# Eight zero products instead of ten at the start, and the half tile ahead of the single tile

## The chip, the cores and the metric

The kernel runs on one core of a Trainium2 chip. The metric is the device time of one execution in microseconds, the median over several executions. The engines are TensorE (PE; its weight loads are shown as PEld), VectorE (DVE), ScalarE (ACT), GpSimd (POOL) and SyncE (SP). SP and POOL issue most DMAs. The engines run their own instruction streams and wait for each other through semaphores.

## The reference

Two blocks follow each other. The first is sparse attention over 8 sequences of 576 tokens and 8 heads of 64; half of the heads look at the last 32 positions, the other half at positions of the same class modulo 32. The second is a layer of 8 experts with one expert for each token. A token takes the expert of its own largest logit, or that of the token before it where a local gate says so:

```python
for s in range(S):
    fresh_e = int(np.argmax(logits[b, s]))
    e = fresh_e if s == 0 or local_gate[b, s] < 0.5 else prev_e
    prev_e = e
    h = np.maximum(x[b, s] @ w1[e], 0.0)      # 512 -> 1024
    out[b, s] = p[e] * (h @ w2[e])            # 1024 -> 512, p = softmax of the logits
```

So the number of tokens of each of the eight experts depends on the data; there are 4608 in all. Everything is float32.

## The kernel before, in words

**Attention.** `attention` (line 148) walks over 8 sequences and 4 pairs of heads. In each step it loads q and k of a pair (SP's queue, line 169), multiplies scores on PE (`scores`, L264), takes the exponential on ACT (L268), masks on DVE (L275), multiplies by the values on PE (L288) and divides on DVE (L301, L302). The results are stored to a table of rows in HBM. Ahead of the first scores, `busy(WARM)` (line 186) issues products of a tile of zeros with itself, 128 x 512 in bf16 (L184); they use nothing but the zeroed tile, and nothing uses their results. `WARM` is 10 (line 59).

**Routing.** A `Router` turns the logits into lists of rows: for each expert the numbers of its tokens in tiles of 128. All experts have at least four such tiles in the code path ("two pairs"); what an expert has beyond these 512 rows is counted in halves of 64 rows, and this count, from 0 to 6, is read into registers as the number of an arm.

**Experts.** `Experts.run` (line 797) goes over the experts in order. Two tiles are done together as a pair, in a scheme with seven products in place of eight (`pair_hidden`, L835, and `pair_output`, L871). `rest` (line 999) does the second pair of an expert, and in the middle of it switches to the arm. The arm builds a list `more` of what is still to do: pairs, a single tile of 128 rows (`single`, L926 for the first layer, L937 for the second), a half tile of 64 rows (`half`, L947 for the first layer, L957 to transpose its result, L967 for the second layer). An arm with number 3 has a single and a half tile.

The order of work in an arm is written out by hand. It gathers the rows of the first entry (`gather`, L765, an indirect DMA issued by POOL, from the table in HBM into one tile in SBUF), ends the pair (`part2`), which issues two scatters of results on POOL (L791), and then, for each entry, issues the gather of the entry after it into the same SBUF tile, and does the entry:

```python
for i, r in enumerate(more):
    then = more[i + 1] if i + 1 < len(more) else nxt
    if i + 1 < len(more):
        self.gather(then)
```

Each of `part2`, `single` and `half` also prepares the entry that follows it, its `nxt`: ACT multiplies the gathered rows by their gate (`scale`, L771), PE transposes them (`turn`, L778), ACT copies the result from PSUM (L779), and for a pair DVE makes four differences (`row_sums`, L787). In `single` the scale stands ahead of the first layer, and the turn between the two layers. In `half` the scale stands ahead of the first layer as well; the turn is made in two calls, one for each tile of a pair that follows, the first after the first layer and the second after the transposes L957. ACT does the relu of a first layer (L822), and for the half tile DVE does the other half of it (L953); ACT copies the second layer's result (L938 for the single tile, L973 for the half tile), and a scatter on POOL writes it. SP loads the weights of the expert after the next one (L724, L727) when the last use of a weight tile is over. `steps` are lists of sums of weights on DVE (L732) that are worked off between the parts.

## Time and profile before

| what | value |
|---|---|
| median of 3 runs | 678.8 us (678.07 to 679.64) |
| profiled execution | 679.77 us, its span 678.0 us |
| PE busy | 661.1 us, 97% of the span |
| PE weight loads | 569.3 us |
| DVE, ACT, POOL busy | 353.8, 195.4, 118.4 us |
| single tile's layers L926 and L937 | 29.2 and 28.4 us in all, four tiles |
| half tile's layers L947 and L967 | 14.6 and 14.7 us in all, four half tiles |
| products of zeros, L184 | 5.9 us, 15 of them in the trace, ten of which stand at the start |

The span runs from the first to the last instruction of one profiled execution; the execution's own time has some 1.8 us around it. A row of the timeline gives start, busy time, engine, line, operation, the tiles written and read and the number of instructions merged; in brackets stands how long the engine was idle before it, and who ended that.

### The profile page before, as it was taken

The page shows a single profiled execution, that of the slowest core. Times are in us where ns is not written, and L with a number is a line of the kernel's source. Part 1 is how long each engine was busy: PE and PEld are TensorE (multiplying, and loading weights), DVE is VectorE, ACT ScalarE, POOL GpSimd, SP SyncE. Part 2 cuts the span into 40 slices and gives each one's busy share as a digit, 9 for nine tenths or more (in the row PEclk, how much of TensorE's full clock was granted, in tenths as well). Part 3 has the DMA queues.
Part 4 walks back from the last instruction along what each step waited for, and adds up shares of the span by engine and source line. Part 5 has one row for each costly group of instructions (what it writes and reads, how often), then busy time and mean ns, then how long its engine had stood idle before and what let it go on. Part 6 is the DMA issues. An engine that isn't in the chain of part 4 may idle for free.

```text
span 678.0 us, 14758 instructions
## 1 busy us (share of the span) xinstructions
PE 661.1 (97%) x6019; PEld 569.3 (84%) x6020; DVE 353.8 (52%) x783; ACT 195.4 (29%) x364; POOL 118.4 (17%) x144
## 2 busy tenths in 40 slices
PE   9999999999999999999999999999999999999994
PEld 6887888878999999499979989996799899699493
DVE  6558876856884447126523664560256456422131
ACT  3545445353311221321222222222222222221220
POOL 3431010112022023012011201301011112121001
PEclk9999999999999999999999999999999999999998
DMA  9999877755321082171045226201711712021001
GB/s 323 408 380 325 278 251 254 274 168 196 122 64 54 17 300 66 39 270 57 27 156 170 65 75 241 67 18 40 268 45 54 256 55 74 34 56 42 18 9 37
DMA packets 35800, 95.83 MB, mean 141 GB/s; under 512 B 4790, under 2 KB 11702, under 8 KB 35628
## 3 DMA queue, kind: packets, MB, share of 16 engines
q1 hardware_dynamic: 27164, 71.41, 30.0%
q0 software_dynamic: 7936, 22.38, 10.3%
q8 instruction: 66, 1.08, 0.7%
q14 instruction: 106, 0.87, 0.4%
q10 hardware_dynamic: 528, 0.10, 0.1%
HBM read 74.69 MB, written 19.69 MB: 139 GB/s over the span
## 4 chain that ended last, share of the span: by engine, by line
PE 57%; DMA 1%; issue 1%; DVE 1%; ACT 0%; POOL 0%; POOLq 0%; ACTq 0%
PE lps L835 22%; PE mps L871 21%; PE mps L937 4%; PE mps L967 2%; PE lps L947 2%; PE lps L926 2%; PE xps L778 2%; DMA x<-xd,gi 1%; PE lps L957 0%; POOL out_dram L791 0%; DVE h L958 0%; ACT y L973 0%; ACT x L771 0%; DVE y L823 0%; DVE wt L732 0%
## 5 line engine op out<-in xcount | busy, mean ns | idle before, releaser
L791 POOL DMA_INDIRECT out_dram<-y,tab x40 | 46.2, 1154 | 350.0 <-DVE y L823 245.4
L835 PE MATMUL lps<-tt,ws 128*128 128x128 f32 x768 | 91.5, 275 | 0.0
L835 PEld LDWEIGHTS lps<-tt,ws 128*128 128x128 f32 x768 | 88.5, 192 | 0.2
L871 PE MATMUL mps<-wt,k 128*128 128x256 f32 x384 | 85.7, 380 | 0.0
L871 PEld LDWEIGHTS mps<-wt,k 128*128 128x128 f32 x384 | 72.8, 190 | 9.9
L835 PE MATMUL lps<-xt,w1t 128*128 128x128 f32 x512 | 63.0, 276 | 3.0 <-ACT y L973 1.9
L835 PEld LDWEIGHTS lps<-xt,w1t 128*128 128x128 f32 x512 | 60.4, 192 | 6.5 <-ACT y L973 3.7
L823 DVE TENSOR_TENSOR h<-lps,u 128x512 f32<-128x512 f32 x48 | 33.1, 691 | 57.6 <-PE lps L835 57.4
L871 PE MATMUL mps<-w2t,h 128*128 128x256 f32 x256 | 60.5, 379 | 0.0
L268 ACT ACTIVATE e<-sps 128x576 f32<-128x576 f32 (+1 forms) x64 | 41.6, 651 | 54.8 <-PE sps L264 53.9
L765 POOL DMA_INDIRECT x<-xd,gi x40 | 42.0, 1050 | 81.4 <-PE lps L835 39.0
L871 PEld LDWEIGHTS mps<-w2t,h 128*128 128x128 f32 x256 | 47.4, 190 | 5.8
L264 PE MATMUL sps<-qk 64*128 64x96 f32 (+2 forms) x704 | 50.4, 280 | 0.9 <-issue 0.8
L822 ACT ACTIVATE h<-h 128x512 f32<-128x512 f32 x48 | 30.2, 630 | 70.1 <-DVE h L823 65.2
L264 PEld LDWEIGHTS sps<-qk 64*128 64x128 f32 (+2 forms) x704 | 42.2, 183 | 8.2 <-issue 6.9
L822 ACT ACTIVATE h<-lps 128x512 f32<-128x512 f32 (+1 forms) x28 | 15.6, 562 | 82.2 <-PE lps L835 66.1
L823 DVE TENSOR_TENSOR u<-lps,p 128x512 f32<-128x512 f32 x16 | 11.1, 692 | 53.4 <-PE lps L835 32.9
L771 ACT ACTIVATE x<-x 128x512 f32<-128x512 f32 (+1 forms) x40 | 27.1, 717 | 33.6 <-DMA x<-xd,gi 21.9
L779 ACT COPY xt<-xps 128x512 f32<-128x512 f32 (+1 forms) x38 | 20.3, 565 | 51.1 <-PE xps L778 51.1
L835 PE MATMUL lps<-tt,w1t 128*128 128x128 f32 x256 | 31.3, 275 | 0.0
L835 PE MATMUL lps<-xt,ws 128*128 128x128 f32 x256 | 31.3, 275 | 0.0
L871 PE MATMUL mps<-w2t,k 128*128 128x256 f32 x128 | 30.4, 380 | 0.0
(238 smaller groups left out, 959.3 us busy)
## 6 DMA issues: line engine op xcount, KB each, us to landing
w1t<-in_w_dram SPq DMA_DIRECT2D x7, 2048.0 KB
w2t<-in_w_dram SPq DMA_DIRECT2D x7, 2048.0 KB
qk<-in_qkl_dram SPq DMA_DIRECT2D x16, 592.0 KB
qk<-in_qks_dram SPq DMA_DIRECT2D x16, 576.0 KB
vl<-in_vf_dram SPq DMA_DIRECT2D x8, 780.0 KB
vs<-in_vg_dram SPq DMA_DIRECT2D x8, 639.8 KB
xd<-xl SPq DMA_DIRECT2D x12, 288.0 KB
xd<-xs SPq DMA_DIRECT2D x48, 63.0 KB
```

Of the source, the lines that this page charges most:

```text
L264: nc.tensor.matmul(ps[0:m, h, c:c + w], lhsT=t[r, S + j * width:S + j * width + m], rhs=t[r, j * width:j * width + w], start=(u.local and ...
L268: nc.scalar.activation(e[0:kb, :, 0:n], ps[0:kb, :, 0:n], Act.Exp, bias=0.0, scale=1.0 / DH ** 0.5)
L765: self.nc.gpsimd.indirect_dma_start(out=r.x[0:r.m, i], out_offset=None, in_=self.xd[0:r.rows], in_offset=bass.IndirectOffsetOnAxis(ap=r.gi ...
L771: self.nc.scalar.activation(r.x[0:r.m, i, 0:D], r.x[0:r.m, i, 0:D], Act.Copy, scale=r.gate[i][0:r.m])
L778: self.nc.tensor.transpose(ps[:, kk, 0:r.m], r.x[0:r.m, i, kk * P:(kk + 1) * P], self.ident[0:r.m, 0:r.m])
L779: self.nc.scalar.copy(out=r.xt[:, i, :, 0:r.m], in_=ps[:, :, 0:r.m])
L791: s = self.nc.gpsimd.indirect_dma_start(out=self.out, out_offset=bass.IndirectOffsetOnAxis(ap=r.si[i][0:r.m], axis=0), in_=y[0:r.m, i], in ...
L822: relu = lambda o, i: nc.scalar.activation(o, i, Act.Relu)
L823: add = lambda o, i, p: nc.vector.tensor_tensor(o, p, i, op=Alu.add)
L835: nc.tensor.matmul(ps[:, f], lhsT=m[:, kk, f * P:(f + 1) * P], rhs=v[:, kk], start=(start and f == 0 and kk == 0), stop=(kk == 1), skip_gr ...
L871: nc.tensor.matmul(ps[:, 0:256], lhsT=m[:, f], rhs=v[:, f], start=(start and f == 0), stop=(f == 3), skip_group_check=True)
L937: nc.tensor.matmul(ps, lhsT=h[f // 4][:, f % 4], rhs=w.w2[:, f], start=(f == 0), stop=(f == FK - 1))
```

## The change

The number of products of zeros ahead of the first scores goes from 10 to 8. In an arm with both, the list `more` holds the half tile ahead of the single tile. Since a half tile can now be followed by an entry of one tile, `turn` with `only=1` does nothing where the entry has no second tile.

```diff
-WARM = 10
+WARM = 8
...
     def turn(self, r, bank, only=None):
         if r is not None:
-            for i in range(r.n) if only is None else [only]:
+            for i in range(r.n) if only is None else range(only, min(only + 1, r.n)):
...
                 if arm > 3:
                     more.append(rows(spot, e, (4, 5)))
+                if arm % 2:
+                    more.append(rows(spot, e, (4 + arm // 2,), HALF))
                 if arm % 4 > 1:
                     more.append(rows(spot, e, (4 + arm // 4 * 2,)))
-                if arm % 2:
-                    more.append(rows(spot, e, (4 + arm // 2,), HALF))
```

## The prediction

> **What bounds the kernel now.** I read the page first, then the timeline of TensorE (PE) over the expert part, then the timelines of POOL and ACT at the same places, because the page's averages hide which wait ends last where the change works.

> ```profile
> span 678.0 us, 14758 instructions
> ...
> PE 661.1 (97%) x6019; PEld 569.3 (84%) x6020; DVE 353.8 (52%) x783; ACT 195.4 (29%) x364; POOL 118.4 (17%) x144
> ```

> PE works 97% of the span, so what lengthens PE's own sequence, or puts a hole in it, lengthens the kernel; work on other engines counts only where PE waits for it. The change touches two places. The first is the start (PE, PEld and ACT rows of the timeline; columns are start, busy us, engine, line, operation):

> ```profile
> 1.37 4.45 PE L184 MATMUL vps<-warm 128*128 128x512 bf16 x10 [1.37 <-DVE warm L179]
> 5.75 3.43 PE L264 MATMUL sps<-qk 64*128 64x96 f32 x48
> ...
> 6.89 1.32 ACT L268 ACTIVATE e<-sps 128x576 f32<-128x576 f32 x2 [4.23 <-PE sps L264]
> ```

> Ten products of zeros start 0.427 us apart; the first scores follow without a hole. The trace's semaphore events have the first qk load complete at 4.62 us, so the scores wait for the zeros, not for their data.

> The second place is an arm with a single tile and a half tile. PE's timeline shows L926/L937 (single) followed by L947/L957/L967 (half) three times, at 262.7, 455.1 and 617.4 us: experts 0, 4 and 7. Expert 4 in full, PE rows first, then POOL and ACT:

> ```profile
> 455.11 0.60 PE L778 MATMUL xps<-ident,x 128*128 128x128 f32 x4
> 455.55 1.89 PE L871 MATMUL mps<-w2t,k 128*128 128x256 f32 x8
> 457.27 7.31 PE L926 MATMUL lps<-xt,w1t 128*128 128x128 f32 x64
> 464.84 0.46 PE L778 MATMUL xps<-ident,x 64*128 64x64 f32 x4 [0.25 <-ACT x L771]
> 465.32 7.13 PE L937 MATMUL mps<-w2t,h 128*128 128x512 f32 x16
> 472.38 3.65 PE L947 MATMUL lps<-w1t,xt 128*64 128x512 f32 x16
> 475.97 0.66 PE L778 MATMUL xps<-ident,x 128*128 128x128 f32 x4
> ...
> 477.93 3.67 PE L967 MATMUL mps<-w2t,h 128*64 128x256 f32 x32
> 482.07 2.05 PE L835 MATMUL lps<-xt,w1t 128*128 128x128 f32 x16 [0.46 <-ACT y L973]
> ```
> ```profile
> 458.71 1.27 POOL L791 DMA_INDIRECT out_dram<-y,tab  x1 [1.15 <-DVE wt L732]
> 460.28 0.94 POOL L765 DMA_INDIRECT x<-xd,gi  x1 [0.30 <-issue]
> ...
> 464.06 0.72 ACT L771 ACTIVATE x<-x 64x512 f32<-64x512 f32 x1 [7.67 <-DMA x<-xd,gi]
> ```

> The second tile of the arm is gathered behind the pair's last scatter, at 460.28; ACT can scale its rows only at 464.06, 3.78 us later, and ends at 464.78. PE turns them at 464.84. That chain starts when the pair's last product ends and is done 7.5 us after it, and the single tile's first layer (L926, 7.15 us from start to the next operation when nothing stops it, at 340.14) covers all but 0.25 us. **The cover is the length of the first tile's first layer.**

> Two more stretches give me durations: a half tile alone after a pair (expert 6) and a single tile alone (expert 2).

> ```profile
> 582.34 0.46 PE L778 MATMUL xps<-ident,x 64*128 64x64 f32 x4
> ...
> 584.66 3.65 PE L947 MATMUL lps<-w1t,xt 128*64 128x512 f32 x16
> 588.24 0.66 PE L778 MATMUL xps<-ident,x 128*128 128x128 f32 x4
> ```
> ```profile
> 347.29 1.04 PE L778 MATMUL xps<-ident,x 128*128 128x128 f32 x8
> 348.16 7.03 PE L937 MATMUL mps<-w2t,h 128*128 128x512 f32 x16
> 355.03 1.17 PE L835 MATMUL lps<-xt,w1t 128*128 128x128 f32 x9
> ```

> [...] 427 ns per product of zeros, and at the end the granted clock falls to 0.50 at 671.7 us, 3 us after PE's last product. [...]

> **The change, part by part.**

> *Two products of zeros fewer.* 2 x 0.427 = 0.85 us less ahead of the scores, so they start at about 4.9, after the load (4.62). But [...] the pairs of score products come 0.11 us apart only from 6.2 us on, twice that before. The first unit is six pairs; with one 0.32 us start and the rest at 0.22 it ends near 6.4 instead of 6.84, and its exp starts 0.45 us earlier. The chain behind it (exp, mask, values) moves with it: the loads used at 7.59, 9.11 and 11.0 complete at 6.47, 8.36 and 9.95, at least 0.75 us early. I take **-0.45**, between 0 (a load late next) and -0.85 (clock already up).

> *Half before single (three arms).* Only the order changes: each instruction and transfer keeps its size. The turn's new bound lets the half tile's two calls serve a next of one tile: the first turns it, the second issues nothing. Other arms keep their order. From the turn of the first tile in the pair (call it A: 262.69, 455.11, 617.37):
> - L947 starts at A+2.32 (expert 6: 582.34 to 584.66) and the next turn is wanted 3.58 later (584.66 to 588.24): A+5.90.
> - The single tile's gather stands at the same place on POOL: after both scatters. The scatters wait for the same DVE additions, so it is issued at about A+5.2 for experts 0 and 4 (5.17 before), and A+4.96 for expert 7, whose scatter takes 1.0 instead of 1.27 us. The gather has 128 rows instead of 64: gathers of 128 rows complete 3.0 to 3.8 us after issue in the trace, those of 64 rows 2.9 to 3.7, so I add nothing. Issue to scale was 3.67, 3.78 and 2.98 us, the scale 0.72, the turn 0.05 later: A+9.67, A+9.78, A+8.71.
> - PE stands for **3.77, 3.88 and 2.81 us**. Queued behind the turn are L957, L967 and the whole single tile; on ACT the half tile's relu (L822) stands behind the scale, so it isn't early either, and DVE's half of the relu follows ACT's.
> - From the turn: 1.8 to L967 (1.96 before; DVE's relu is up to 0.2 earlier relative to it), 3.6 for L967, 7.15 for L926, 0.87 and 6.87 for turn and L937 (expert 2's rows): 20.3. The next pair then starts at A+29.95, 30.06 and 28.99; it was 26.85, 26.96 and 26.54. Per expert **+3.1, +3.1 and +2.45**.
> - In that sum are the gains: the 0.46 us wait for ACT's y copy at the end of a half tile goes in all three (a single tile's end shows none at 355.03), the 0.25 and 0.14 us waits of the old second turn go, and the half tile's turn in the pair is 0.05 us shorter.
> - SP's weight loads follow the last use of the weights: w1 is free 1.6 us earlier before the next pair, w2 0.5 us later; neither was waited for by PE in these stretches: nothing. Expert 0's remaining weight sums on DVE now run beside L967 and L926: nothing.

> Sum: 3.1 + 3.1 + 2.45 - 0.45 = **+8.2 us**. The profiled execution took 679.77 (span 678.0, 1.77 around it), 0.97 over the median of 678.8; I put the sum on the median: **687.0**, and about 686.2 for a span.

> **Rivals.**
> 1. *The clock falls in the hole (28%).* A stand of 3.8 us is longer than the 3.0 us of idleness after which the clock fell at the end[...]. For: the clock's record at 671.7; against: no hole of this length lies inside the span. One time 688.7, two 690.4.
> 2. *A faster transfer (14%).* If the gather takes expert 7's 2.98 us everywhere and POOL its shorter scatter, the holes shrink by about 1 us each in experts 0 and 4, or somewhat more if the single's rows come sooner: 683 to 685.
> 3. *The hole is covered after all, faster (4%).* Place: the turn at A+5.90. If the scaled rows are there by then, only gains remain: 26.18 against 26.85, 26.96 and 26.54, so -1.8, and -0.45 at the start: 676.5. It decides at 0.7 us from gather issue to scaled rows, where 3.7 to 4.5 were seen; or if the gather went ahead of the scatters, which its order in the queue excludes.
> 4. *The new order isn't executed (2%).* Then only the start counts: 678.35. Three stretches in the timeline speak against it.

> **How the numbers follow.** The main case has 52%, own range 685.2 to 688.2 (holes 0.5 us either way, start 0 to -0.85). About 0.2%, 1.4 us, is what a measurement can tell from no change. Slower by more: main, 1 and 2, 94%; within: 2%; faster: 4%. Range 683.5 to 690.0: it leaves out rival 3, two clock falls, and the lower part of rival 2.

> **What would show it.** PE rows in expert 4: L778 (64 rows), L871, L947, then L778 with a wait of 3 to 4 us put down to ACT x L771 or the DMA behind it; L967, L926, L937, and L835 with no wait for ACT y. PE's busy time is hardly changed, its share falls by a point. First scores near 4.9, first exp near 6.45. Wrong if the wait is under 2 us, if the gather is issued before the scatters, or if L947 outlasts the scale.

## The result and the profile after

The changed kernel takes 693.4 us, median of 6 runs (692.45 to 694.4), against 678.8 us for 6 runs of the kernel before (677.38 to 679.64): a ratio of 1.0223, 95% interval 1.0212 to 1.0234. It is 14.6 us slower. The forecast was slower, by 8.2 us, 687.0 in all, and its range ended at 690.0: the sign was right, the size was not. The profiled execution took 694.4 us, its span 692.7.

The page after, first lines and the slice line of the granted clock (one digit for each fortieth of the span, in tenths):

```profile
span 692.7 us, 14737 instructions
...
PE 667.3 (96%) x6017; PEld 573.9 (83%) x6018; DVE 353.9 (51%) x783; ACT 195.8 (28%) x364; POOL 116.5 (17%) x144
...
PEclk9999999999999998999999999998999999998998
```

The span is 14.7 us longer, but PE's busy time also grew, by 6.2 us (661.1 before), though PE has no more work than before (two products of zeros fewer). Three slices ahead of the last one show an 8. Work that takes longer at a lower clock is a second loss beside the waiting.

The waits of PE after (engine, line, releaser: us in all, times, longest) show the first loss:

```profile
PE xps L778 <- ACT x L771: 10.1, 3, 3.4
PE mps L967 <- DVE h L958: 1.6, 3, 0.5
```

Three times PE stands for 3.4 us ahead of a turn, as the main case said; the wait of 0.5 us ahead of L967 was not foreseen. Here is one whole arm (expert 0), on PE's timeline, then POOL's and ACT's row of the second tile's rows:

```profile
261.85 0.46 PE L778 MATMUL xps<-ident,x 64*128 64x64 f32 x4
262.24 1.99 PE L871 MATMUL mps<-w2t,k 128*128 128x256 f32 x8
264.16 3.65 PE L947 MATMUL lps<-w1t,xt 128*64 128x512 f32 x16
271.24 1.12 PE L778 MATMUL xps<-ident,x 128*128 128x128 f32 x4 [3.43 <-ACT x L771]
272.15 1.06 PE L957 MATMUL lps<-ident,h 128*128 128x128 f32 x4
273.73 5.11 PE L967 MATMUL mps<-w2t,h 128*64 128x256 f32 x32 [0.52 <-DVE h L958]
278.76 7.41 PE L926 MATMUL lps<-xt,w1t 128*128 128x128 f32 x64
...
293.75 1.95 PE L835 MATMUL lps<-xt,w1t 128*128 128x128 f32 x16
```
```profile
267.08 0.99 POOL L765 DMA_INDIRECT x<-xd,gi  x1 [0.30 <-issue]
```
```profile
270.46 0.72 ACT L771 ACTIVATE x<-x 128x512 f32<-128x512 f32 x1 [7.75 <-DMA x<-xd,gi]
```

The order is the predicted one: the gather of the single tile is issued 5.23 us after the arm's first turn, ACT scales 3.38 us later, and L947 had ended at 267.8. But L967 takes 5.11 us, where it took 3.67 before, and the second turn and the transposes L957 are slower too (1.12 and 1.06 us, where they took 0.66 and 0.90). The same stretch cut at the changes of the clock (columns: stretch, length, busy time and instructions of PE, PEld, DVE, ACT and POOL, then the granted clock, DMA share and GB/s):

```profile
262.50:266.43 3.93, 3.93 (x20) 2.02 (x21) 3.30 (x7) 0.21 (x1) 2.14 (x2) 1.00 0.18 67
266.43:269.84 3.41, 1.38 (x8) 0.21 (x4) 0.00 (x0) 0.00 (x0) 1.33 (x2) 1.00 0.48 151
269.84:271.24 1.40, 0.00 (x1) 0.00 (x1) 0.00 (x0) 0.78 (x2) 0.00 (x0) 0.50 0.03 12
271.24:276.67 5.43, 4.91 (x22) 3.29 (x24) 3.25 (x6) 1.18 (x3) 0.00 (x0) 0.50 0.00 0
276.67:280.00 3.33, 3.33 (x31) 2.36 (x28) 0.00 (x0) 1.09 (x3) 0.08 (x1) 1.00 0.00 0
```

At 269.84, while PE stands, the granted clock falls to 0.50; it comes back at 276.67, 6.83 us later. The other two arms do the same: down at 467.82 and 635.07, up 6.83 us later each time. The mean granted clock of the six executions is 0.981 to 0.986, against 0.994 to 0.997 in all twenty of the kernel with fewer zeros alone (below), so the clock fell in the others too.

From the arm's first turn to the next pair's first product:

| arm of expert | before | after | added |
|---|---|---|---|
| 0 | 26.85 | 31.90 | 5.05 |
| 4 | 26.96 | 32.11 | 5.15 |
| 7 | 26.54 | 32.25 | 5.71 |

Together 15.9 us. Outside the arms the profile after gets some 1.5 us back: it reaches the first arm 0.84 us earlier (261.85 against 262.69; only 0.04 of this comes from the start, most of the rest from shorter waits between 60 and 145 us), two waits of 0.56 us elsewhere are gone, and one of 0.47 is new. That leaves 14.4 of the span's 14.7; the last 0.3 was not followed.

At the start, PE's and ACT's rows after:

```profile
1.36 3.59 PE L184 MATMUL vps<-warm 128*128 128x512 bf16 x8 [1.36 <-DVE warm L179]
4.89 4.25 PE L264 MATMUL sps<-qk 64*128 64x96 f32 x48
```
```profile
6.53 0.65 ACT L268 ACTIVATE e<-sps 128x576 f32<-128x576 f32 x1 [3.87 <-PE sps L264]
```

The scores start at 4.89, the first exponential at 6.53 (4.9 and 6.45 were forecast). The values of the first unit are done at 10.62, though, against 10.66 before: in this execution the clock rose at 7.02 instead of 6.16, which takes the lead back.

### The profile page after: what moved, and what is told of

Read it like the earlier page. It is cut to its first block, busy times and chain, and to the rows that moved or that the text cites. A ratio compares the mean times of both kernels' runs of the same rounds, so it can differ in the third digit from the quotient of the medians.

```text
span 692.7 us, 14737 instructions
## 1 busy us (share of the span) xinstructions
PE 667.3 (96%) x6017; PEld 573.9 (83%) x6018; DVE 353.9 (51%) x783; ACT 195.8 (28%) x364; POOL 116.5 (17%) x144
## 3 DMA queue, kind: packets, MB, share of 16 engines
q8 instruction: 66, 1.08, 0.7%
## 4 chain that ended last, share of the span: by engine, by line
PE 92%; DVE 2%; DMA 2%; issue 1%; ACT 1%; POOL 0%; POOLq 0%; SPq 0%; DVEq 0%; ACTq 0%
PE lps L835 29%; PE mps L871 28%; PE sps L264 6%; PE vps L288 6%; PE lps L926 4%; PE mps L937 4%; PE tps L330 3%; PE mps L967 3%; PE xps L778 3%; PE sps L258 2%; DMA x<-xd,gi 1%; PE tps L354 1%; PE vps L184 1%; DMA xd<-xl 1%; PE tps L382 1%
## 5 line engine op out<-in xcount | busy, mean ns | idle before, releaser
L791 POOL DMA_INDIRECT out_dram<-y,tab x40 | 46.1, 1152 | 368.7 <-DVE y L823 247.4
L835 PE MATMUL lps<-tt,ws 128*128 128x128 f32 x768 | 91.7, 275 | 0.5 <-issue 0.5
L835 PEld LDWEIGHTS lps<-tt,ws 128*128 128x128 f32 x768 | 88.6, 192 | 0.7 <-issue 0.5
L871 PE MATMUL mps<-wt,k 128*128 128x256 f32 x384 | 85.7, 380 | 0.0
L871 PEld LDWEIGHTS mps<-wt,k 128*128 128x128 f32 x384 | 72.8, 190 | 9.9
L835 PEld LDWEIGHTS lps<-xt,w1t 128*128 128x128 f32 x512 | 60.6, 192 | 4.0 <-issue 2.7
L835 PE MATMUL lps<-xt,w1t 128*128 128x128 f32 x512 | 62.7, 276 | 0.5 <-ACT y L973 0.5
L871 PE MATMUL mps<-w2t,h 128*128 128x256 f32 x256 | 60.5, 379 | 0.0
L268 ACT ACTIVATE e<-sps 128x576 f32<-128x576 f32 (+1 forms) x64 | 41.7, 651 | 53.2 <-PE sps L264 52.2
L765 POOL DMA_INDIRECT x<-xd,gi x40 | 40.2, 1005 | 79.9 <-PE lps L835 44.0
L871 PEld LDWEIGHTS mps<-w2t,h 128*128 128x128 f32 x256 | 47.4, 190 | 5.8
L264 PE MATMUL sps<-qk 64*128 64x96 f32 (+2 forms) x704 | 51.0, 283 | 0.1
L822 ACT ACTIVATE h<-h 128x512 f32<-128x512 f32 x48 | 30.2, 630 | 70.1 <-DVE h L823 67.1
L264 PEld LDWEIGHTS sps<-qk 64*128 64x128 f32 (+2 forms) x704 | 43.1, 186 | 8.2 <-issue 6.0
L822 ACT ACTIVATE h<-lps 128x512 f32<-128x512 f32 (+1 forms) x28 | 15.8, 565 | 92.9 <-PE lps L835 68.3
L787 DVE TENSOR_TENSOR tt<-xt 128x256 f32<-128x256 f32 x32 | 13.5, 421 | 52.2 <-ACT xt L779 52.2
L771 ACT ACTIVATE x<-x 128x512 f32<-128x512 f32 (+1 forms) x40 | 27.1, 717 | 35.4 <-DMA x<-xd,gi 23.0
L835 PE MATMUL lps<-tt,w1t 128*128 128x128 f32 x256 | 31.3, 275 | 0.0
L835 PE MATMUL lps<-xt,ws 128*128 128x128 f32 x256 | 31.3, 275 | 0.0
```

What stands on the lines that cost most here:

```text
L264: nc.tensor.matmul(ps[0:m, h, c:c + w], lhsT=t[r, S + j * width:S + j * width + m], rhs=t[r, j * width:j * width + w], start=(u.local and ...
L268: nc.scalar.activation(e[0:kb, :, 0:n], ps[0:kb, :, 0:n], Act.Exp, bias=0.0, scale=1.0 / DH ** 0.5)
L765: self.nc.gpsimd.indirect_dma_start(out=r.x[0:r.m, i], out_offset=None, in_=self.xd[0:r.rows], in_offset=bass.IndirectOffsetOnAxis(ap=r.gi ...
L771: self.nc.scalar.activation(r.x[0:r.m, i, 0:D], r.x[0:r.m, i, 0:D], Act.Copy, scale=r.gate[i][0:r.m])
L791: s = self.nc.gpsimd.indirect_dma_start(out=self.out, out_offset=bass.IndirectOffsetOnAxis(ap=r.si[i][0:r.m], axis=0), in_=y[0:r.m, i], in ...
L822: relu = lambda o, i: nc.scalar.activation(o, i, Act.Relu)
```

## The experiments

All medians are set against runs of the kernel before on the same chip; intervals are 95%.

| kernel | median us | ratio to before |
|---|---|---|
| zeros alone | 678.05 | 0.9996 [0.9985, 1.0006] |
| order alone | 693.72 | 1.0221 [1.0194, 1.0248] |
| hole filled, 8 float32 products | 695.99 | 1.0245 [1.0223, 1.0267] |
| hole filled, 4 float32 products | 691.07 | 1.0175 [1.0147, 1.0202] |
| hole filled, 2 float32 products | 690.82 | 1.0189 [1.0172, 1.0206] |
| hole filled, 1 float32 product | 691.98 | 1.0190 [1.0161, 1.0218] |
| hole filled, 14 products of zeros | 685.77 | 1.0107 [1.0088, 1.0125] |
| new order, gathers early | 676.75 | 0.9963 [0.9950, 0.9977] |
| old order, gathers early | 677.99 | 0.9988 [0.9978, 0.9999] |
| no products of zeros | 686.01 | 1.0108 [1.0076, 1.0139] |

### Which half of the change it is

The kernel before with `WARM = 8`, and the changed kernel with `WARM = 10`.

> Eight zero products, the old order in the arm. Theory: the start alone is worth 0.1 to 0.5 us, 678.5 us; in the profile the first scores start near 4.9 us and the first exp before 6.6, with no clock fall inside the span. Rival: the start is worth the whole 0.85 us and more (the changed kernel stood 0.84 us ahead when its first arm began), 677.9 or less.

> Ten zero products, the half tile ahead of the single tile. Theory: all of the loss is in the order of the arm: 693.4 to 694.2 us, with three holes of 3.3 to 3.5 us ahead of the turn in the half tile, and a clock fall of 6.8 us at each. Rival: part of the loss comes from the array being less warm at the start: below 692 us.

The order alone gives 693.72, all of the loss. The zeros alone give 678.05, with an interval on both sides of no change, which is too wide to choose between the two expectations. The order-alone profile has the holes again (3.48, 3.53 and 3.32 us) and three falls of the clock, of 3.41, 6.83 and 6.83 us; 6.8 us had been expected at each.

### Does filling the hole keep the clock up?

Unused products between the half tile's first layer and the turn that waits, only where the next entry has one tile. They leave the wait itself alone and only change what PE does in it.

```diff
             nc.vector.tensor_scalar(flat[:, 256:], a[:, 256:], 0.0, None, Alu.max)
+            if nxt is not None and nxt.n == 1:
+                ps = bank()
+                for _ in range(8):
+                    nc.tensor.matmul(ps, lhsT=w.w1[:, 0, 0:P], rhs=w.w1[:, 0, 0:512], start=True, stop=True, skip_group_check=True)
             self.turn(nxt, bank, 0)
```

> The changed kernel with eight unused products (128x512, fp32, 0.43 us each) ahead of the turn in the half tile that precedes a single tile. They fill the hole but cannot shorten it, as the turn still waits for the scaled rows. Theory: 7.4 of the 14.6 us lost are the clock at half rate after each hole, so with a busy array the clock stays up (mean 0.995) and the time is 686 us. Rival: the new order is slow in itself (waits between L957, L967 and L926 that the hole only starts): 692 to 694 us with the clock at 0.995.

The median rose to 695.99, and this by itself refutes nothing, because the fill was mis-sized. A float32 product of 512 columns is two instructions (16 records for eight products), so eight of them took twice the time planned:

```profile
263.53 3.65 PE L947 MATMUL lps<-w1t,xt 128*64 128x512 f32 x16
267.12 7.13 PE L957 MATMUL xps<-w1t 128*128 128x512 f32 x16
274.09 0.60 PE L778 MATMUL xps<-ident,x 128*128 128x128 f32 x4
```

The turn came at 274.09 - 261.22 = 12.87 us into the arm instead of 9.39, 3.5 us late in each of three arms. The clock did not fall in any of them, and 695.99 - 10.5 is 685.5. With the size corrected to four products:

> The changed kernel with four unused products ahead of the waiting turn. Eight took 6.97 us, twice what was planned for them, so four take 3.5 us, as long as the hole. Theory: clock at 0.995, and 693.4 less the 7.4 us of the clock falls: 686 us. Rival: something besides the clock makes the stretches behind the hole slow: 690 us or more.

The arms now read 29.68, 29.79 and 29.59 us with no fall in them, against 31.90, 32.11 and 32.25: 7.2 us less in all. So the stretches behind the hole aren't slow in themselves. The total, 691.07, missed the expectation all the same: it is only 2.3 us lower. This profile (692.1 us) has a stop elsewhere, in the middle of a run of the same products, which no semaphore explains ("issue", time in which the engine waited for nothing that the profile shows):

```profile
407.55 1.58 PE L835 MATMUL lps<-xt,w1t 128*128 128x128 f32 x12
412.00 1.22 PE L835 MATMUL lps<-xt,w1t 128*128 128x128 f32 x4 [2.87 <-issue]
```

That stop, the fall of the clock that follows it (3.41 us at half rate) and one of 1.08 us at 546.7 take back about 5.6 us. The fastest of its four runs was 687.78, at a mean clock of 0.996. The two others, 691.0 and 691.14, have 0.993, which is an estimated 4 us more at half rate (0.003 of 690 us, twice); where isn't known. Smaller fills were to find how much idleness the clock bears:

> The changed kernel with two unused products (1.74 us) ahead of the waiting turn, so that 1.7 us of the hole stay empty, at most half of a clock window of 3.41 us. Theory: the clock falls only after a window that is idle for the larger part (the falls seen had 59 to 84% of their window idle): no falls, 686 us, clock 0.995. Rival: half a window of idleness is enough, falls at some of the three holes: 688 to 693 us, clock 0.981 to 0.99.

> The changed kernel with one unused product (0.87 us) ahead of the waiting turn; 2.6 us of the hole stay empty. Theory: as the clock windows lie anywhere against the hole, the idle share of the worst window is between 38 and 76%, so the clock falls at some of the holes and not at others: 687 to 691 us, clock 0.984 to 0.993, changing from run to run. Rival: only a window that is idle nearly throughout brings the clock down, then none falls: 686 us.

With two products 1.65, 1.57 and 1.35 us of the holes stay empty, and the profile (687.84 us) has no fall between its start and end. It is the exception: the three other runs took 690.7 to 691.25 at a mean clock of 0.990 against its 0.996, an estimated 8 us at half rate (0.006 of 689 us, twice), so the clock fell in them, as the rival expectation had it. Where isn't recorded. The hole and the 0.52 us wait behind it lie within 3.33 us (269.83 to 273.16 in the first arm), so a window that takes in both is idle for 2.17 of 3.41 us, not for half of it; the stops named above are another candidate. With one product 2.45, 2.45 and 2.24 us stay empty, and the clock falls in all three arms, for 6.83, 3.41 and 3.41 us; the mean clock runs from 0.983 to 0.992, and the median of 691.98 lies 1 us above the range expected.

Because the float32 fills left these loose ends, the last fill uses another kind of work and a finer size: 14 products of zeros in bf16 (a zeroed tile of its own, set by POOL). They were planned at 0.213 us each, half of the 0.427 at half rate; in the trace they start 0.216 us apart.

```diff
+            moe.zero = keep.tile([P, 512], BF16, name="zero")
+            nc.gpsimd.memset(moe.zero, 0.0)
...
+            if nxt is not None and nxt.n == 1:
+                ps = bank()
+                for _ in range(14):
+                    nc.tensor.matmul(ps, lhsT=self.zero[:, 0:P], rhs=self.zero, start=True, stop=True, skip_group_check=True)
             self.turn(nxt, bank, 0)
```

> The changed kernel with 14 products of zeros (bf16, 128 x 512, unused) ahead of the waiting turn of the half tile: 14 x 0.213 = 2.98 us of the holes of 3.43, 3.40 and 3.29 us are PE's work, and 0.3 to 0.45 us of each stay empty, so nothing is held up. Clock theory (the falls follow PE's idleness): no fall in the three arms, arms of about 29.65 us from turn to next pair, some 7.4 us less than the changed kernel: 686.0. If half rate had another cause, or the loss were in the order: the clock still falls and it stays at 693.4. If the kind of product matters (bf16 of zeros doesn't count as work): the same 693.4.

685.77, with runs from 685.0 to 686.11, all at a mean clock of 0.995 or 0.996. PE's timeline of the first arm (the added lines shift the numbers by two to six; 13 of the 14 products left a record):

```profile
261.51 0.46 PE L780 MATMUL xps<-ident,x 64*128 64x64 f32 x4
...
263.82 3.65 PE L949 MATMUL lps<-w1t,xt 128*64 128x512 f32 x16
267.64 2.97 PE L959 MATMUL xps<-zero 128*128 128x512 bf16 x13 [0.16 <-issue]
270.95 0.66 PE L780 MATMUL xps<-ident,x 128*128 128x128 f32 x4 [0.34 <-ACT x L773]
271.44 0.68 PE L963 MATMUL lps<-ident,h 128*128 128x128 f32 x4
272.63 3.67 PE L973 MATMUL mps<-w2t,h 128*64 128x256 f32 x32 [0.52 <-DVE h L964]
...
291.23 0.94 PE L837 MATMUL lps<-xt,w1t 128*128 128x128 f32 x7
```

The turn comes as late as ever, 270.95 - 261.51 = 9.44 us after the first one, and the rows come no sooner. But the second layer takes 3.67 us again, the clock record has no fall between the start and the end of the program, and the arms take 29.72, 29.79 and 29.51 us. Work that nobody uses, done in a wait, saves 7.2 us in the three arms (96.26 less 89.02). By the medians it is 693.4 - 685.8 = 7.6, or 6.9 where each is set against the kernel before that ran beside it. What remains, 7.8 us over before, comes with the hole.

### What the order costs when the rows are there

Here the second tile of the arm is gathered into the other slot of the `x` tile right behind the first, ahead of the pair's end and its scatters, with either order of the tiles.

```diff
-                    more.append(rows(spot, e, (4 + arm // 4 * 2,)))
+                    more.append(rows(spot, e, (4 + arm // 4 * 2,), at=len(more)))
...
+                if arm == 3:
+                    self.gather(more[1])
...
-                    if i + 1 < len(more):
+                    if i + 1 < len(more) and arm != 3:
```

(`at` is the first slot that `gather`, `scale`, `turn` and the gate use; 0 elsewhere.) First the new order, then the old one, both with 8 zeros:

> The changed kernel with the single tile's rows gathered into the second half of the SBUF tile, ahead of the pair's two scatters on POOL rather than behind them. Theory: the hole comes only from the place of this gather in POOL's queue; without it the gains of the order remain (no wait of 0.46 us at the arm's end, 0.25 and 0.14 us waits gone): 676.5 to 677.5 us, no clock fall. Rival: half before single costs time apart from the gather: 679 us or more.

> Eight zero products, the old order (single, then half), the half tile's rows gathered ahead of the pair's scatters into the second half of the SBUF tile. Theory: with neither order short of rows, only the waits of 0.25 and 0.14 us go against the same kernel with the late gather (678.05): 677.7 us, and half first with the early gather (676.75) stays about 1 us ahead, mostly by two waits of 0.56 us at the ends of arms without further tiles. Rival: the order is worth nothing and the early gather is all: 676.7 us.

The new order with early gathers takes 676.75, the fastest of all, with an interval below no change. The arm's PE and ACT rows:

```profile
261.07 0.46 PE L778 MATMUL xps<-ident,x 64*128 64x64 f32 x4
261.46 1.99 PE L871 MATMUL mps<-w2t,k 128*128 128x256 f32 x8
263.38 3.65 PE L947 MATMUL lps<-w1t,xt 128*64 128x512 f32 x16
266.97 0.66 PE L778 MATMUL xps<-ident,x 128*128 128x128 f32 x4
267.57 0.89 PE L957 MATMUL lps<-ident,h 128*128 128x128 f32 x4
268.98 3.67 PE L967 MATMUL mps<-w2t,h 128*64 128x256 f32 x32 [0.52 <-DVE h L958]
272.59 7.41 PE L926 MATMUL lps<-xt,w1t 128*128 128x128 f32 x64
...
287.58 1.95 PE L835 MATMUL lps<-xt,w1t 128*128 128x128 f32 x16
```
```profile
261.83 0.72 ACT L771 ACTIVATE x<-x 128x512 f32<-128x512 f32 x1
```

ACT scales the single's rows at 261.83, so the turn at 266.97 waits for nothing and the hole is gone. The arms take 26.51 us each. In the old order with early gathers they take 26.54, 26.55 and 26.55, and in the kernel with the zeros alone (old order, late gather) 26.67, 26.55 and 26.55. So with the rows there in time the order itself is worth 0.03 or 0.04 us an arm: the 0.46 us wait for ACT's y at the end of the arm has gone, and a 0.52 us wait ahead of L967 has come. The old order with early gathers, 677.99, can't be told from the zeros alone, 678.05: its waits of 0.25 and 0.14 us, seen in the profile before, are hardly there in the profile of the zeros alone, so there was little to remove. The 1.2 us between the two orders is mostly outside these arms: waits of 0.56 us at 404.3 and 531.3 us in the kernel with the zeros alone (405.7 and 532.6 in the old order with early gathers) are not there in the new one. Why they go is not settled.

### What the zeros at the start are worth at all

The kernel before with `WARM = 0`:

> The kernel before without any product of zeros at the start. If the number of zeros hardly matters because the cold stretch only moves: scores start near 4.65 as the load lands[...], and the end is within 1 us of before, 678 to 679.5. If the zeros shorten the cold stretch under the scores: two pairs more of scores and values at half rate, up to +2 us, 680 to 681.

Neither expectation held: 686.01, with runs from 683.39 to 687.39. Its start, and two stops later on (PE's timeline):

```profile
4.88 5.44 PE L264 MATMUL sps<-qk 64*128 64x96 f32 x48 [4.88 <-DMA qk<-in_qkl_dram]
10.25 2.32 PE L288 MATMUL vps<-vl,e 128*64 128x65 f32 x48
12.50 0.43 PE L258 MATMUL sps<-maskS,identb 126*126 126x252 bf16 x2
```
```profile
243.85 1.62 PE L835 MATMUL lps<-xt,w1t 128*128 128x128 f32 x6 [2.66 <-issue]
...
297.55 0.60 PE L835 MATMUL lps<-xt,w1t 128*128 128x128 f32 x4 [1.88 <-issue]
```

The clock rises only at 11.80 us, and the first unit is done at 12.50 instead of 10.66: 1.84 us, which is the second expectation. The rest is 4.5 us in the two stops and a fall of the clock at 243.91, right behind the first of them (PE is busy for 0.75 of the 3.41 us before the fall). The stops are of the same kind as the one with four float32 products: no semaphore, in the first products of a pair, the DMA engines full (share 1.03 and 0.98 in the windows of 3.41 us that hold them). What holds PE there is not shown, nor whether the missing zeros brought it about or a mere shift of the code did.

## Why the prediction failed, point by point

**The main case was right, in mechanism and size.** With the clock held up by zeros, the arms take 29.72, 29.79 and 29.51 us, against 29.95, 30.06 and 28.99 forecast, and the total is 7.8 us over before against 8.2. That the sums agree so closely is partly luck. The arms' errors, -0.2, -0.3 and +0.5 us, are those of the gather's time and cancel; outside the arms two waits of 0.56 us went that nobody had forecast, while the 0.45 us of the start can't be seen in its own experiment. The cover is the first tile's first layer; a half tile's layer, half as long, can't cover a gather that is issued behind two scatters. The gather took 3.38, 3.36 and 3.53 us from issue to scale (3.67, 3.78 and 2.98 were taken over): the short one of expert 7 did not come back at that place, where it took 3.53. The 20.3 us from the second turn to the next pair measured 20.28 (291.23 - 270.95).

**The step that failed is the weighing of rival 1, the clock.** It was named, at the right place, but given 28%, priced at 1.7 us a time (688.7 less 687.0) and counted twice at most, so that two falls were left out of the range. The changed kernel shows a fall in every arm, at a price of 7.2 / 3 = 2.4 us each (31.90 - 29.72 = 2.2, 32.11 - 29.79 = 2.3 and 32.25 - 29.51 = 2.7). The chance went wrong because the text compared the length of the hole with 3.0 us, the idleness after which the clock fell at the program's end. The price was the author's estimate: no trace of before shows how long the clock stays down.

| kernel | clock fell at the window's end | clock stayed |
|---|---|---|
| before | 88% (end of the program) | |
| changed | 60, 72, 84% (the arms), 89% (end of the program) | |
| 1 float32 product | 64, 50, 66% (the arms) | |
| 2 float32 products | | 44, 46% |
| no products of zeros | 78% (240.50 to 243.91) | 55% (295.10 to 298.52) |

In the changed kernel and the one before, no other window of full clock has more than 18% idle. Here are the two window rows that stand nearest each other among the fills, one float32 product first, then two, with the grid of each run (columns as above):

```profile
468.34:471.75 3.41, 1.69 (x14) 1.22 (x16) 0.85 (x2) 1.95 (x4) 0.00 (x0) 1.00 0.00 0
```
```profile
465.05:468.46 3.41, 1.84 (x11) 0.92 (x9) 0.42 (x1) 1.17 (x3) 0.00 (x0) 1.00 0.25 73
```

PE is busy 1.69 of 3.41 us in the first, and the clock falls at 471.75; it is busy 1.84 in the second, and the clock stays. A hole of 3.4 us, wherever it lies on the grid, puts 1.7 us or more into one window: from these shares I estimate a fall nearly every time, not one in four.

The return took a busier window. In the three arms of the changed kernel the window after the fall still holds the end of the hole and, in the second and third, the 0.52 us wait: 42, 42 and 28% idle. The clock stayed down behind each, though a window of 44, 46 or 55% above did not bring it down, and came back behind the next, with 14, 0 and 0% idle: 6.83 us instead of 3.41. That is why a fall cost 2.4 us on average. Where one window was enough, in the second and third arm with one float32 product (31.45 and 30.80 us), it cost 1.7 and 1.3. Without zeros at the start it stayed down even after a window (4.98 to 8.39 us) in which the first scores keep PE busy throughout by the profile, and came back at the end of the next, 11.80. So PE's busy time in the profile does not tell every return.

**Terms of the sum that were off.** The step from the turn to L967 was put at 1.8 us. It took 1.68 behind the hole with the clock up (272.63 - 270.95) and 2.01 with early gathers (268.98 - 266.97). In both it holds a wait that the prediction didn't have: the second call of the turn had stood in the time in which DVE copies h (L958), and where it issues nothing, PE waits 0.52 us. This is the gain of 0.46 us at the arm's end, given back. L926 took 7.25 us instead of 7.15, so the 20.3 us came out because small errors cancel. The three waits listed as gains are indeed gone, and the order's own worth, with early gathers in both, is 0.04 us an arm or less.

The start was put at -0.45, between 0 and -0.85. The profiles with eight zeros have the clock rising anywhere from 4.12 to 7.02 us, and the first unit's end at 10.05 to 10.62 against 10.66: 0.04 to 0.6 us gained. In several of them the values then wait 0.3 us for their load, which had been taken to be early enough. The interval of the zeros alone (-1.0 to +0.4 us) does not tell this from nothing.

**The other rivals.** The faster transfer didn't come (3.4 to 3.5 us). The covered hole is what early gathers make: 676.75 against its price of 676.5, reached partly for other reasons, since 1.1 us of it are waits elsewhere. The order is executed as written.

## What to carry to other kernels

Before two pieces of work change places, ask what each of them covers: here the longer first layer covered a gather, and the shorter one left a hole. Price a hole of PE at its length and at the clock: where a window of 3.41 us was less than half busy, the clock fell at its end in nine of the ten cases above, at a cost of 1.3 to 1.7 us for one window at half rate and 2.2 to 2.7 for two. Small waits close behind a hole add to it: here 0.52 us, in the window behind the fall of two arms. Cure the cause (an earlier gather into a free slot brought 676.75), and where that can't be had, put cheap products into the wait: here 14 products of zeros kept the clock up (7.2 us).

## What the runs showed of the hardware beyond that

- A float32 product of 128 x 512 was two instructions and took 0.87 us at full clock (8 products, 16 records, 6.97 us), a bf16 one of zeros 0.216.
- PE stood inside a run of products with no semaphore in sight, while the DMA engines were nearly full: 2.87 us with four float32 products (share 0.98 from 406 to 412.5 us), 2.66 and 1.88 us without zeros (1.03 and 0.98 in the windows of 3.41 us that hold them). Full DMA engines alone did not bring it about: from 536 to 540 us of the kernel before the share is 1.00, and PE is busy for all of the 4 us. As each kernel was profiled once, it isn't shown whether the edit or the single execution decides. Behind two of these stops the clock fell too (2.87 us with four float32 products, 2.66 without zeros). With their falls the stops took about 5.6 and 4.5 us in these two profiles, so a difference of this size between two kernels whose traces have not been laid side by side may be only this.
